# Band scores of a local-attention block: from one 128-row matmul per head pair with zero-filled queries to two 64x64 tiles of the TensorE array

## The chip, the core and the metric

The kernel runs on one core of one Trainium2 chip. The metric is device microseconds of one execution; lower is better. The value for the kernel before is the median of three runs. The trace that is read here comes from one further execution of the same program, taken by the hardware profiler.

## What is computed

Three parts follow each other: an attention with a downsampled and a local branch, and two MLPs. In the local branch a query sees only the seven keys around it (three on each side), which is the "band".

```
# attention: B=4, H=8, S=576, D=64, factor=4
q_d, k_d, v_d = means of q, k, v over groups of 4 positions      # 144 positions
out_up    = repeat(softmax(q_d k_d^T / sqrt(D)) v_d, 4)
mask      = |i - j| < 4
out_local = softmax(where(mask, q k^T / sqrt(D), -1e9)) v
x  = out_up + out_local             # as 2304 tokens x 512
h  = relu(x @ w_in);  x = (h*h) @ w_out        # 512 -> 2048 -> 512
h  = x @ w_in2;       out = softplus(h) @ w_out2
```

## The kernel before

The 2304 tokens are worked on in five blocks of 8, 6, 8, 8 and 6 units of 64 queries. A unit of 64 queries is a `local` task in the first two blocks (14 tasks), and half of a `direct` task, which works on VectorE without TensorE scores, in the other three. The downsampled branch is made of `pooled` tasks, one for a batch and a pair of heads. The MLP steps are `hidden` (its matmuls write `ph`) and `outputs` (they write `y`); each weight is split into two fp32r parts by ScalarE and VectorE (`raw`, `f`, `r`, `w`) the first time it comes in. The MLP inputs and hidden values are split likewise (`xh` and `xl`, `gh` and `gl`).

The order of the instructions of each engine is fixed when the program is built. Each task is a generator that asks for an engine and names an estimated duration, and `Order.run` always takes the piece that could start first. The scores of a `local` task are entered with 0.86 us of TensorE. DMAs on the SP queue are entered in the planner's estimate of when they land (`order.landed`), which also moves what is planned behind them. SP's DMAs use eight semaphores in turn, and each of them waits until the DMA that used its semaphore before it (eight places back) has landed.

A `local` task for 64 queries and 4 pairs of heads goes: scores `lsc` (TensorE), scaling and mask into `ls` (VectorE), row maximum `ln` (VectorE), exponentials `le` with row sums (ScalarE), sum and reciprocal, scaling, transposes `lpp` (TensorE), their copy `lpt`, product with the values `lav` (TensorE), addition of the upsampled branch `lt` (VectorE), and the split into `xh` and `xl`.

For the scores the two heads of a pair lie on partitions 0 to 63 and 64 to 127. So that one matmul with 128 rows yields both heads, the query tile is block-diagonal: head 0 has its 64 queries in columns 0 to 63 and zeros below, head 1 its queries in columns 64 to 127 and zeros above. The zeros are written once by GpSimd. Queries of one task and one pair (index `w`, eight of them in a tile that serves two tasks) are not adjacent: the tile is stored as query by `w`, so that the stationary operand `q[:, :, w]` steps by eight elements. The moving operand is the 70 keys of the unit, read as 96 columns (`KWP`), of which the last 26 are not used. One fp32 matmul is recorded as two passes, each a weight load and a matmul, so that a task's four matmuls are eight rows of each kind.

The names `first` and `w_first` in rows are the same key and query tiles where they lie in borrowed buffers during the start.

Of the kernel before, what the change touches and what calls it, by code (L numbers as in the profile page):

```python
# [9 lines left out]
F32 = mybir.dt.float32  # L10
# [7 lines left out]
B, H, S, D = 4, 8, 576, 64  # L18
NP = H // 2
# [5 lines left out]
QB = 64  # L25
NBLK = S // QB
NG = B * NBLK
KW = QB + 2 * (FCT - 1)
KWP = 96
KH = SP // 2  # L30
NF = DFF // 128
NEG = -1.0e9
# [22 lines left out]
for run in RUNS:  # L55
    b = run[1] + run[0] * NB
# [24 lines left out]
BUFS = dict(q=2, v=3, s=3, e=4, t=5, vd=2, pt=2, n=6, do=5)  # L81
# [36 lines left out]
class Event:  # L118
    at = None
# [129 lines left out]
def fused_kernel(ctx: ExitStack, tc: tile.TileContext, lq, lk, lv, dqk, dv, cdmask, pqk, pv, wts, cmask, cdiag, cident, out):  # L249
    nc = tc.nc  # L250
    act, dve, pe, sp = nc.scalar, nc.vector, nc.tensor, nc.sync
# [34 lines left out]
    r_up = ring(att, "up", [128, NP, SP], 2)  # L286
    banded = lstack.enter_context(tc.tile_pool(name="banded", bufs=1))
    r_v = ring(banded, "v", [KH, 1024], BUFS["v"])
    qs = [banded.tile([128, 2, 2 * NP * QB], F32, name=f"q{k}", tag=f"q{k}") for k in range(BUFS["q"])]
    ks = [banded.tile([128, 2 * NP * KW + KWP - KW], F32, name=f"k{k}", tag=f"k{k}") for k in range(BUFS["q"])]  # L290
    r_q = Ring(lambda name: qs[len(r_q.taken) % BUFS["q"]], BUFS["q"])
    r_k = Ring(lambda name: ks[len(r_k.taken) % BUFS["q"]], BUFS["q"])
    r_t = ring(banded, "t", [128, NP * QB], BUFS["t"])
    r_h = ring(psum, "h", [128, 512], 2)
    r_y = [ring(psum, f"y{m}", [128, 512], 1) for m in range(4)]
# [2 lines left out]
    order = Order()  # L298
# [130 lines left out]
    for g, (i, j) in enumerate(g_block):  # L429
        p0, p1 = LOCAL[i]  # L430
# [15 lines left out]
    lent, first_bufs = {}, {}  # L446

    def lend():

        for p in range(LENT):  # L450
            k = SLOTS1 - 1 - p
            lent[k] = Host()
            both = wpool.tile([128, 2048], F32, name=f"w_first{k}", tag=f"w{k}")
            x, y = both[:, :1024], both[:, 1024:]
            if p < NP:
                q = x.rearrange("p (a x) -> p a x", a=2)
                nc.gpsimd.memset(q, 0.0)
                first_bufs["q", p] = Guest(q, lent[k])
                first_bufs["v", p] = Guest(y[:KH], lent[k])
            else:  # L460
                first_bufs["pv", 0] = Guest(x[:KH], lent[k])
        for p, r in enumerate((r_xh[1], r_xl[1])):
            b = r.take("first")
            host = Host(b)
            x = b.tile.bitcast(F32).rearrange("p h n -> p (h n)")
            first_bufs["in", 2 + p] = Guest(x[:, :2 * S], host)
            k = x[:, 2 * S:2 * S + 2 * NP * KW + KWP - KW]
            nc.gpsimd.memset(k[:, 2 * NP * KW:], 0.0)
            first_bufs["k", p] = Guest(k, host)

    def take_for(r, kind, at):
        return first_bufs.get((kind, at)) or r.take(kind)
# [22 lines left out]
    def load_tasks():  # L495
        todo = [(mask, cmask)]
        for x, y in ((diag, cdiag), (ident, cident)):
            t = yield "sp", 0.06
            sp.dma_start(out=x, in_=y)
            order.landed(t, 65536)  # L500
        for (kind, at, hp, i, _), ev in zip(tasks, arrived, strict=True):
            if kind == "d":
                continue
            if kind == "l":
                if at % 2 == 0:
                    two = at // 2
                    t = yield "sp", 0.06, *room(r_q, "q", two), *room(r_k, "k", two), *room(r_v, "v", two)
                    bq, bk, bv = (take_for(r, x, two) for r, x in ((r_q, "q"), (r_k, "k"), (r_v, "v")))
                    for x in (bq, bk, bv):
                        x.left = 2  # L510
                    for hh in range(2):
                        p0 = 64 * hh
                        sp.dma_start(out=bq.tile[p0:p0 + 64, hh, :], in_=lq[at // 2, p0:p0 + 64])
                        order.landed(t, 128 << 10)
                        t = yield "sp", 0.06
                    sp.dma_start(out=bk.tile[:, :2 * NP * KW], in_=lk[at // 2])
                    there = order.landed(t, 256 * NP * KW * 4)
                    t = yield "sp", 0.06
                    sp.dma_start(out=bv.tile[:KW], in_=lv[at // 2])
                    vthere = order.landed(t, KW * 4096)  # L520
                ev.buf = bq, bk, bv, at % 2
                ev.at = there
                ev.v.at = vthere
            else:
                two = at * NP + hp
                t = yield "sp", 0.06, *room(r_in, "in", two)
                ev.buf = take_for(r_in, "in", two)
                sp.dma_start(out=ev.buf.tile, in_=pqk[at * NP + hp])
                ev.at = order.landed(t, 128 * 4 * 2 * S)
                late = i in DIRECT  # L530
                t = yield "sp", 0.06, *room(r_in if late else r_v, "pv", two)
                ev.v.buf = take_for(r_in if late else r_v, "pv", two)
                ev.v.tile = ev.v.buf.tile[:KH, :1024]
                sp.dma_start(out=ev.v.tile, in_=pv[at * NP + hp])
                ev.v.at = order.landed(t, KH * 4096)
                if todo:
                    t = yield "sp", 0.06
                    sp.dma_start(out=mask, in_=cmask)
                    order.landed(t, 128 * 12 * KW)
                    todo = []  # L540
# [110 lines left out]
    def local(g, banks, ev, pace):  # L651

        b, blk = divmod(g, NBLK)
        i, j = g_block[g]
        t = yield "pe", 0.86, ev, pace, banks, r_s, r_e, r_n, r_t
        sc, s, e, n, o = bank(banks, "lsc"), r_s.take("ls"), r_e.take("le"), r_n.take("ln"), r_t.take("lt")
        bq, bk, bv, at = ev.buf
        q = bq.tile.rearrange("p a (q w) -> p (a q) w", w=2 * NP)
        sc4 = sc.tile[:, :NP * KWP].rearrange("p (h k) -> p h k", h=NP)
        for h in range(NP):  # L660
            w = at * NP + h
            pe.matmul(sc4[:, h, :], q[:, :, w], bk.tile[:, w * KW:w * KW + KWP],  # L662
                      start=True, stop=True)
        used_once(t, bq, bk)
        t = yield "dve", t_dve(280)
        var = 0 if blk == 0 else 2 if blk == NBLK - 1 else 1
        s3 = s.tile[:, :NP * KW].rearrange("p (h k) -> p h k", h=NP)
        dve.scalar_tensor_tensor(
            out=s3, in0=sc4[:, :, :KW], scalar=1.0 / D ** 0.5,
            in1=mask[:, var, :].unsqueeze(1).to_broadcast([128, NP, KW]), op0=ALU.mult, op1=ALU.add)  # L670
        sc.free = t
        t = yield "dve", t_dve(280)
# [315 lines left out]

    with tc.manual_schedule():
        lend()  # L990
        for x in qs + ks:
            nc.gpsimd.memset(x, 0.0)
        act.preload_act_table_set("natural_log_exp_and_others")
        order.spawn(load_tasks(), -100)
        order.spawn(load_weights(), 0, 8.0)
# [21 lines left out]
def _layout(q, k, v, moe_w_in, moe_w_out, moe2_w_in, moe2_w_out):  # L1017
# [9 lines left out]
    kp[..., halo:halo + S] = kt  # L1027
    vs = np.zeros((B, S + 2 * halo, NP, 128), f4)
    vs[:, halo:halo + S] = np.asarray(v, f4).reshape(B, NP, 2, S, D).transpose(0, 3, 1, 2, 4).reshape(B, S, NP, 128)
    lq = np.zeros((NG // 2, 128, QB, 2, NP), f4)  # L1030
    lk = np.zeros((NG // 2, 128, 2, NP, KW), f4)
    lv = np.zeros((NG // 2, KW, 2, NP * 128), f4)
    for b in range(B):
        for i in range(NBLK):
            g = b * NBLK + i
            at = g // 2, slice(None), g % 2
            lq[g // 2, :, :, g % 2] = qt[b, :, :, i * QB:(i + 1) * QB].transpose(1, 2, 0)
            lk[at] = kp[b, :, :, i * QB:i * QB + KW].transpose(1, 0, 2)
            lv[at] = vs[b, i * QB:i * QB + KW].reshape(KW, NP * 128)
    pqk = np.concatenate([qt.reshape(B * NP, 128, S), kt.reshape(B * NP, 128, S)], axis=2)  # L1040
# [55 lines left out]
```

## Time and profile before

| | |
|---|---|
| median of 3 runs | 935.39 us (934.44 to 937.53) |
| the profiled execution | 939.24 us, of which the span from the first to the last instruction is 937.5 us and 1.74 us lie around it |
| busy in the span | PE 911.1 us, weight loads 786.4, DVE 641.8, ACT 508.9, POOL 76.9 |
| HBM traffic | 179.49 MB moved, mean 191 GB/s |
| `lsc` in the chain that ended last | 2% of the span |

PE is TensorE's matmuls, PEld its weight loads, DVE is VectorE, ACT ScalarE, POOL GpSimd, SP the queue that issues most DMAs. A busy time counts an instruction from start to end, and matmuls overlap in the pipeline, so the pace of PE is read from one start to the next. In rows of a timeline the first number is the start and the second the stretch until the last of the merged instructions ended; the bracket gives the idle time ahead and what ended it.

### The profile page before, as it was taken

The numbers are of one execution on the slowest core, as the hardware profiler recorded it, in microseconds if no ns is written. First come the engines' busy times: TensorE is split into PE (matmuls) and PEld (weight loads), VectorE is DVE, ScalarE is ACT, GpSimd is POOL, SyncE is SP. The second block draws the span as 40 slices with busy tenths as digits, with TensorE's granted clock in tenths as the row PEclk, the third lists the DMA queues.
The fourth block names the chain that finished last, engine by engine and source line by source line (L and its number), as shares of the span: only waits on it lengthen the run. The fifth ranks groups of instructions, "written<-read, shape, count | busy, mean of one in ns | idle before, by whom it ended". The sixth has DMA issues, their size and how long they took to land.

```text
span 937.5 us, 12449 instructions
## 1 busy us (share of the span) xinstructions
PE 911.1 (97%) x4416; PEld 786.4 (84%) x4416; DVE 641.8 (68%) x1105; ACT 508.9 (54%) x1141; POOL 76.9 (8%) x146
## 2 busy tenths in 40 slices
PE   4899999999999999999999999999999999999998
PEld 3777888999888877898888888888999888988886
DVE  3768889889999989998797998997211225223222
ACT  3657677667687877654444544443333325444443
POOL 2000000000000000021111112110220011010000
PEclk9969999999999999999999999999999999999999
DMA  8826977986685667378776587661772154123101
GB/s 210 235 75 209 285 258 233 326 278 232 213 306 195 225 239 263 139 259 289 252 257 203 164 275 260 218 212 51 248 248 89 45 165 150 46 90 128 41 0 46
DMA packets 50202, 179.49 MB, mean 191 GB/s; under 512 B 5874, under 2 KB 6258, under 8 KB 50140
## 3 DMA queue, kind: packets, MB, share of 16 engines
q1 hardware_dynamic: 31132, 109.48, 34.8%
q0 software_dynamic: 19008, 69.21, 22.8%
q8 instruction: 35, 0.57, 0.2%
q14 instruction: 27, 0.22, 0.1%
HBM read 140.40 MB, written 38.27 MB: 191 GB/s over the span
## 4 chain that ended last, share of the span: by engine, by line
PE 82%; DVE 9%; DMA 5%; ACT 2%; issue 1%; POOL 0%; SPq 0%; ACTq 0%; POOLq 0%; DVEq 0%
PE ph L870 37%; PE y L924 36%; DMA raw<-wts 3%; DMA first<-lk 3%; PE lsc L662 2%; PE pqk L566 2%; PE ppo L631 1%; PE lav L699 1%; DVE vd L626 1%; DVE f L378 1%; PE psc L589 1%; DVE f L382 1%; DVE gl L319 1%; DVE w L319 1%; PE lpp L691 1%
## 5 line engine op out<-in xcount | busy, mean ns | idle before, releaser
L870 PE MATMUL ph<-xh,w 128*128 128x512 f32 (+2 forms) x1304 | 398.4, 368 | 1.2 <-DVE g L893 1.2
L870 PEld LDWEIGHTS ph<-xh,w 128*128 128x128 f32 x1304 | 242.0, 189 | 33.1 <-DVE g L893 2.3
L870 PE MATMUL ph<-xl,w 128*128 128x512 f32 (+2 forms) x652 | 238.3, 365 | 0.2 <-DVE xl L319 0.2
L924 PE MATMUL y<-gh,w 128*128 128x512 f32 (+2 forms) x656 | 200.2, 367 | 0.0
L924 PE MATMUL y<-w,gh 128*128 128x512 f32 x576 | 179.6, 393 | 0.0
L319 DVE TENSOR_TENSOR gl<-g,gh 128x512 fp32r<-128x512 f32 (+2 forms) x163 | 102.0, 626 | 89.4 <-ACT gh L304 88.4
L870 PEld LDWEIGHTS ph<-xl,w 128*128 128x128 f32 x652 | 123.1, 189 | 15.9 <-DVE xl L319 0.4
L413 POOL DMA_DIRECT2D w<-wdram x132 | 70.1, 534 | 793.9 <-ACT g L887 387.6
L924 PEld LDWEIGHTS y<-gh,w 128*128 128x128 f32 x656 | 121.1, 188 | 14.4 <-issue 0.3
L924 PEld LDWEIGHTS y<-w,gh 128*128 128x128 f32 x576 | 106.7, 188 | 20.6
L924 PE MATMUL y<-gl,w 128*128 128x512 f32 (+2 forms) x328 | 119.1, 363 | 0.0
L924 PE MATMUL y<-w,gl 128*128 128x512 f32 x288 | 112.9, 392 | 0.2 <-DVE gl L319 0.2
L893 DVE SCALAR_TENSOR_TENSOR g<-ph,g 128x512 f32<-128x512 f32 (+2 forms) x81 | 50.8, 628 | 90.4 <-ACT g L891 90.3
L304 ACT ACTIVATE gh<-g 128x512 fp32r<-128x512 f32 (+2 forms) x125 | 71.6, 572 | 70.9 <-PE y L924 51.9
L887 ACT ACTIVATE g<-ph 128x512 f32<-128x512 f32 (+2 forms) x81 | 44.5, 549 | 116.7 <-PE ph L870 107.8
L882 ACT ACTIVATE g<-ph 128x512 f32<-128x512 f32 (+2 forms) x82 | 44.5, 543 | 113.3 <-PE ph L870 92.9
L924 PEld LDWEIGHTS y<-gl,w 128*128 128x128 f32 x328 | 61.7, 188 | 7.1 <-issue 0.3
L924 PEld LDWEIGHTS y<-w,gl 128*128 128x128 f32 x288 | 54.0, 188 | 12.5 <-DVE gl L319 1.0
L369 ACT ACTIVATE f<-raw 128x512 f32<-128x512 f32 x64 | 42.5, 666 | 19.9 <-DMA raw<-wts 11.3
L306 DVE CAST gh<-g 128x512 fp32r<-128x512 f32 (+2 forms) x38 | 15.6, 411 | 49.5 <-PE y L924 43.5
L762 DVE TENSOR_TENSOR prod<-dqk 128x896 f32<-128x896 f32 x44 | 47.7, 1085 | 1.3 <-DMA dqk<-dqk 1.0
L885 ACT ACTIVATE g<-g 128x512 f32<-128x512 f32 (+2 forms) x82 | 47.4, 578 | 1.9
(103 smaller groups left out, 1035.0 us busy)
## 6 DMA issues: line engine op xcount, KB each, us to landing
w<-wdram POOLq DMA_DIRECT2D x132, 512.0 KB, 4.2
raw<-wts SPq DMA_DIRECT2D x64, 512.0 KB, 5.3
wdram<-w SPq DMA_DIRECT2D x64, 512.0 KB, 5.7
dqk<-dqk SPq DMA_DIRECT2D x11, 896.0 KB, 8.2
in<-pqk SPq DMA_DIRECT2D x14, 576.0 KB, 4.8
dv<-dv SPq DMA_DIRECT2D x11, 640.0 KB, 3.9
out<-o SPq DMA_DIRECT2D x18, 256.0 KB, 2.5
pv<-pv SPq DMA_DIRECT2D x15, 288.0 KB
```

What stands on the lines that cost most here:

```text
L304: act.activation(out=out, in_=in_, func=AF.Copy, scale=scale)
L319: dve.tensor_tensor(out=out, in0=whole, in1=high.bitcast(F32), op=ALU.subtract)
L369: act.activation(out=f.tile, in_=high.bitcast(F32), func=AF.Abs, scale=REBIAS)
L413: nc.gpsimd.dma_start(out=weights[slot][:, half], in_=wdram[c, half])
L566: pe.matmul(src, ident, x4[:, :, :, k], start=(k == 0), stop=(k == FCT - 1))
L762: dve.tensor_tensor(out=p4, in0=k4[:, :, tok:tok + TAPS, :], in1=q4[:, tok].unsqueeze(2).to_broadcast([128, 2, TAPS, D]), op=ALU.mult)
L870: pe.matmul(ph.tile[:, :n], w, y, start=(k == 0), stop=(k == len(prs) - 1))
L882: act.activation(out=o, in_=h, func=AF.Relu)
L885: act.activation(out=o, in_=o, func=AF.Square)
L887: act.activation(out=o, in_=h, func=AF.Abs)
L893: dve.scalar_tensor_tensor(out=o, in0=h, scalar=0.0, in1=o, op0=ALU.max, op1=ALU.add)
L924: pe.matmul(o, wt, y, start=(begin and k == 0), stop=(end and k == 2))
```

## The change: two 64x64 tiles, contiguous queries, 70 keys

The zeros, the padding of the keys and the GpSimd memsets are dropped. Each head's scores become a matmul of its own: 64 stationary rows (the head's dimensions) by 64 query columns, over 70 moving key columns. Head 0 uses partitions 0 to 63 for its operands and its output, head 1 partitions 64 to 127, so that the two are different 64x64 tiles of the array; both write the same PSUM bank. The 64 queries of a set now lie side by side. The queries of two tasks come in one DMA of 128 partitions in place of two of 64. What VectorE reads of the scores is as many elements as before.

```diff
-    qs = [banded.tile([128, 2, 2 * NP * QB], F32, name=f"q{k}", tag=f"q{k}") for k in range(BUFS["q"])]
-    ks = [banded.tile([128, 2 * NP * KW + KWP - KW], F32, name=f"k{k}", tag=f"k{k}") for k in range(BUFS["q"])]
+    r_q = ring(banded, "q", [128, 2 * NP * QB], BUFS["q"])
+    r_k = ring(banded, "k", [128, 2 * NP * KW], BUFS["q"])
...
-                    for hh in range(2):
-                        p0 = 64 * hh
-                        sp.dma_start(out=bq.tile[p0:p0 + 64, hh, :], in_=lq[at // 2, p0:p0 + 64])
-                        order.landed(t, 128 << 10)
-                        t = yield "sp", 0.06
-                    sp.dma_start(out=bk.tile[:, :2 * NP * KW], in_=lk[at // 2])
+                    sp.dma_start(out=bq.tile, in_=lq[at // 2])
+                    order.landed(t, 256 << 10)
+                    t = yield "sp", 0.06
+                    sp.dma_start(out=bk.tile, in_=lk[at // 2])
...
-        q = bq.tile.rearrange("p a (q w) -> p (a q) w", w=2 * NP)
-        sc4 = sc.tile[:, :NP * KWP].rearrange("p (h k) -> p h k", h=NP)
+        q = bq.tile.rearrange("p (w q) -> p w q", q=QB)
+        sc4 = sc.tile[:, :NP * KW].rearrange("p (h k) -> p h k", h=NP)
         for h in range(NP):
             w = at * NP + h
-            pe.matmul(sc4[:, h, :], q[:, :, w], bk.tile[:, w * KW:w * KW + KWP],
-                      start=True, stop=True)
+            for p in (slice(0, 64), slice(64, 128)):
+                pe.matmul(sc4[p, h], q[p, w], bk.tile[p, w * KW:w * KW + KW], start=True, stop=True)
...
-            out=s3, in0=sc4[:, :, :KW], scalar=1.0 / D ** 0.5,
+            out=s3, in0=sc4, scalar=1.0 / D ** 0.5,
...
-        for x in qs + ks:
-            nc.gpsimd.memset(x, 0.0)
```

On TensorE the order of all instructions stays as it was, and only the scores take another form. Before, the last three `local` tasks of the first block stand ahead of the first MLP step like this:

```order
L699 MATMUL lav<-lpt,w_first_92 128x128 x4
L662 MATMUL lsc<-k_81,w_first_92 128x96 x4
L662 MATMUL lsc<-k_82,w_first_94 128x96 x8
L870 MATMUL ph<-xh,w_83 128x256
L870 MATMUL ph<-xl,w_83 128x256
```

With the change the same place reads:

```order
L690 MATMUL lav<-lpt,w_first_86 128x128 x4
L654 MATMUL lsc<-k,w_first_86 64x70 x8
L654 MATMUL lsc<-k,w_first_87 64x70 x16
L861 MATMUL ph<-xh,w_79 128x256
L861 MATMUL ph<-xl,w_79 128x256
```

Each of the three tasks has eight matmuls of half the rows and columns in place of four, at the same place between `lav` and `ph`.

On the SP queue the loads of the first pair of tasks stand behind those of the first pooled tasks. Before:

```order
L534 DMA pv<-pv 72x1024
L513 DMA w_first_88<-lq 64x512 x2
L516 DMA first<-lk 128x560
L519 DMA w_first_88<-lv 70x1024
L528 DMA first<-pqk 128x1152
```

With the change:

```order
L525 DMA pv<-pv 72x1024
L504 DMA w_first_84<-lq 128x512
L507 DMA first<-lk 128x560
L510 DMA w_first_84<-lv 70x1024
L519 DMA first<-pqk 128x1152
```

One DMA fewer stands ahead of the keys, with as many bytes, and what follows moves up one place in the turn of the eight semaphores.

VectorE's list is the same for its first 196 rows. Then, at the last tasks of the second block, some fifty rows come in another order, since the planner's times of the loads moved. Before:

```order
L710 TENSOR_TENSOR lt<-lav,up 64x256 x2
L319 TENSOR_TENSOR w_1298<-f,w_1298 128x512
L306 CAST gh<-g 128x512
L319 TENSOR_TENSOR xl<-lt,xh 128x4x64
L319 TENSOR_TENSOR gl<-g,gh 128x512
L668 SCALAR_TENSOR_TENSOR ls<-lsc,mask 128x280
```

With the change:

```order
L701 TENSOR_TENSOR lt<-lav,up 64x256
L303 CAST w_1335<-f 128x512
L701 TENSOR_TENSOR lt<-lav,up 64x256
L659 SCALAR_TENSOR_TENSOR ls<-lsc,mask 128x280
L303 CAST xh<-lt 128x4x64
```

The mask of the next scores now stands ahead of the split of the task before. Over the whole program VectorE has two `xh` casts and one `lpt` copy more, and two `gh` casts and one `part` copy less; ScalarE the reverse. Behind this place the lists agree again.

## Rows read from the trace of the kernel before

**Rows 1.** The page: busy time of the engines and their shares of the span.

```profile
PE 911.1 (97%) x4416; PEld 786.4 (84%) x4416; DVE 641.8 (68%) x1105; ACT 508.9 (54%) x1141; POOL 76.9 (8%) x146
```

**Rows 2.** Windows: stretch: its length, each engine's busy us (instructions), PEclk, DMA share, GB/s.

```profile
60.00:142.00 82.00, 81.61 (x422) 66.73 (x422) 67.24 (x158) 58.45 (x196) 0.00 (x0) 0.97 0.71 226
142.00:232.00 90.00, 89.83 (x501) 85.71 (x500) 81.03 (x154) 62.17 (x125) 0.00 (x0) 1.00 0.78 268
232.00:358.40 126.40, 123.06 (x581) 102.52 (x579) 119.91 (x208) 96.86 (x211) 0.00 (x0) 1.00 0.69 243
358.40:937.50 579.10, 574.79 (x2736) 494.36 (x2736) 338.46 (x509) 259.47 (x495) 70.11 (x132) 1.00 0.49 163
```

**Rows 3.** The chain in order of time around 350 us: start, us, what.

```profile
349.54 5.79 DMA raw<-wts
...
357.67 0.70 DVE g L893
...
358.42 3.06 PE ph L870 x12
```

**Rows 4.** The view of line 662 (the scores): who waited for it, us, times.

```profile
  DVE ls L668: 6.0, 7
```

**Rows 5.** Weight loads by form: rows*columns, operand, count, busy us, mean ns.

```profile
L662 PEld LDWEIGHTS lsc<-k,q 128*128 128x128 f32 x48 | 11.8, 332 | 0.1
...
L691 PEld LDWEIGHTS lpp<-ident,le 128*70 128x70 f32 x56 | 7.3, 134 | 1.7 <-issue 1.0
L699 PEld LDWEIGHTS lav<-lpt,v 70*128 70x128 f32 x48 | 6.2, 191 | 0.4
```

**Rows 6.** Timeline of PE between 100 and 119 us.

```profile
100.78 0.90 PE L589 MATMUL psc<-qkd,qd 128*96 128x144 f32 x6
101.52 2.07 PE L662 MATMUL lsc<-k,q 128*128 128x96 f32 x8
103.37 0.47 PE L870 MATMUL ph<-xh,w 128*128 128x512 f32 x1
...
115.16 0.41 PE L617 MATMUL ppp<-ident,pe 96*72 96x96 f32 x3
115.41 1.08 PE L699 MATMUL lav<-lpt,v 70*128 70x128 f32 x8
116.33 2.04 PE L662 MATMUL lsc<-k,q 128*128 128x96 f32 x8
118.15 0.48 PE L924 MATMUL y<-gh,w 128*128 128x512 f32 x1
```

**Rows 7.** Timeline of PE between 35 and 62 us.

```profile
35.38 1.65 PE L589 MATMUL psc<-qkd,qd 128*96 128x144 f32 x6
36.83 0.69 PE L617 MATMUL ppp<-ident,pe 96*72 96x96 f32 x3
...
52.25 3.79 PE L699 MATMUL lav<-lpt,w_first 70*128 70x128 f32 x16
55.83 5.86 PE L662 MATMUL lsc<-k,w_first 128*128 128x96 f32 x24
61.40 0.56 PE L870 MATMUL ph<-xh,w 128*128 128x256 f32 x1
```

**Rows 8.** Timeline of all engines in the start.

```profile
28.92 2.19 PE L662 MATMUL lsc<-first,w_first 128*128 128x96 f32 x8 [1.92 <-DMA first<-lk]
...
43.00 0.45 DVE L668 SCALAR_TENSOR_TENSOR ls<-lsc,mask 128x280 f32<-128x280 f32 x1 [1.32 <-PE lsc L662]
...
46.40 1.91 DVE L626 TENSOR_REDUCE vd<-pv 72x256 f32<-72x1024 f32 x1
...
48.45 2.26 PE L631 MATMUL ppo<-ppt,vd 72*128 72x288 f32 x4 [1.96 <-DVE ln L682]
```

**Rows 9.** Two windows of the start, columns as in rows 2.

```profile
3.00:28.00 25.00, 13.10 (x50) 10.95 (x50) 12.90 (x23) 9.91 (x40) 4.29 (x8) 1.00 0.94 226
...
57.00:60.00 3.00, 3.00 (x14) 3.00 (x14) 2.25 (x7) 1.34 (x5) 0.00 (x0) 0.50 0.00 0
```

More of the change, by code (lines that the diff above doesn't have):

```diff
@@ L28 @@
 KW = QB + 2 * (FCT - 1)
-KWP = 96
 KH = SP // 2
@@ L288, in fused_kernel @@
     r_v = ring(banded, "v", [KH, 1024], BUFS["v"])
-    qs = [banded.tile([128, 2, 2 * NP * QB], F32, name=f"q{k}", tag=f"q{k}") for k in range(BUFS["q"])]
-    ks = [banded.tile([128, 2 * NP * KW + KWP - KW], F32, name=f"k{k}", tag=f"k{k}") for k in range(BUFS["q"])]
-    r_q = Ring(lambda name: qs[len(r_q.taken) % BUFS["q"]], BUFS["q"])
-    r_k = Ring(lambda name: ks[len(r_k.taken) % BUFS["q"]], BUFS["q"])
+    r_q = ring(banded, "q", [128, 2 * NP * QB], BUFS["q"])
+    r_k = ring(banded, "k", [128, 2 * NP * KW], BUFS["q"])
     r_t = ring(banded, "t", [128, NP * QB], BUFS["t"])
@@ L455, in lend @@
             if p < NP:
-                q = x.rearrange("p (a x) -> p a x", a=2)
-                nc.gpsimd.memset(q, 0.0)
-                first_bufs["q", p] = Guest(q, lent[k])
+                first_bufs["q", p] = Guest(x[:, :2 * NP * QB], lent[k])
                 first_bufs["v", p] = Guest(y[:KH], lent[k])
@@ L466, in lend @@
             first_bufs["in", 2 + p] = Guest(x[:, :2 * S], host)
-            k = x[:, 2 * S:2 * S + 2 * NP * KW + KWP - KW]
-            nc.gpsimd.memset(k[:, 2 * NP * KW:], 0.0)
-            first_bufs["k", p] = Guest(k, host)
+            first_bufs["k", p] = Guest(x[:, 2 * S:2 * S + 2 * NP * KW], host)
     def take_for(r, kind, at):
@@ L1029, in _layout @@
     vs[:, halo:halo + S] = np.asarray(v, f4).reshape(B, NP, 2, S, D).transpose(0, 3, 1, 2, 4).reshape(B, S, NP, 128)
-    lq = np.zeros((NG // 2, 128, QB, 2, NP), f4)
+    lq = np.zeros((NG // 2, 128, 2, NP, QB), f4)
     lk = np.zeros((NG // 2, 128, 2, NP, KW), f4)
@@ L1036, in _layout @@
             at = g // 2, slice(None), g % 2
-            lq[g // 2, :, :, g % 2] = qt[b, :, :, i * QB:(i + 1) * QB].transpose(1, 2, 0)
+            lq[at] = qt[b, :, :, i * QB:(i + 1) * QB].transpose(1, 0, 2)
             lk[at] = kp[b, :, :, i * QB:i * QB + KW].transpose(1, 0, 2)
```

## The prediction, as it was made before the run

> **What bounds the kernel now.** I read the page first: PE is busy for 911.1 of 937.5 us, the next engine, DVE, for 641.8 [rows 1]. That says TensorE, but the share is an average, so I cut the span into four stretches [rows 2]. From 358 us on PE is busy for 574.8 of 579.1 us and DVE for 338.5: there TensorE alone counts, and the change touches nothing in it. From 232 to 358 us DVE is busy for 119.9 of 126.4 us, so that only 6.5 us of it are idle, and the chain of waits up to 358.42 runs over loads of weights and VectorE (`raw`, then `g`, then `ph`) [rows 3]. Ahead of that, from 60 to 232 us, PE is packed (171.4 of 172 us) and DVE idles for 14.8 and 9.0 us. All 14 tasks that the change touches lie before 142 us, eight of them before 61 us. So a gain is made where PE is packed, has to pass a stretch in which VectorE is the bound, and is then kept to the end.
>
> **What the scores cost.** A task's scores are eight passes. From their start to the start of what follows is 1.85 us at 101.52 and 1.82 us at 116.33, 0.23 us a pass [rows 6]. Three tasks at 55.83 take 5.57 us for 24 passes, again 0.23 [rows 7], although the granted clock is 0.50 there [rows 9], the level of 1.2 GHz. Other matmuls follow the clock: `psc` with 144 columns takes 0.242 us a pass at 35.38 [rows 7] and 0.123 at 100.78 [rows 6], `lav` 0.224 and 0.115. So it is not the array that sets the 0.23 us. The weight loads tell what does: those of `lsc`, whose 128 columns step by eight elements, take 332 ns, those of `lav`, 128 columns side by side, 191 [rows 5]. I read it that the stepped read of the queries is the bound. The `psc` rows at 35.38 also show the lower level of the clock, as slow as at 57, though the column of the windows [rows 9] reads 1.00 in the start; I trust the durations.
>
> **What they will cost.** The stepped read goes, and each task has 16 passes of 64 weight columns and 70 moving columns. By `psc`, 0.123 us for 144 columns, a pass streams 60 ns at 2.4 GHz and 118 ns at 1.2 GHz. A load of 64 side by side fits under it: `lav` holds a load of 128 in its 0.115 us. The trace has no tiled matmul, so the price has two ends. If the two heads of a pair run at once, 8 x 60 ns = 0.48 us a task; if one after the other, 16 x 60 = 0.96; if every pass costs as much as the shortest in the trace, `ppp` with 0.25 us for three, 16 x 83 ns = 1.33. I take the middle of the first two, 0.72, since the passes of one head stand one behind the other and can only overlap where the heads change. To this comes the change of the array's form, twice a task. When `y` starts at 118.15, 0.22 us of the scores (2.04 less 1.82) are still in flight [rows 6]; if they have to end first, on both sides, that is 0.44 us; nothing at the least, and I take 0.3. A rule for it is in the Trainium skill, TensorEngine Tiling (Array Packing), Tiling Modes: changing the tiling mode, not just the tile, drains the array. By that rule the full 0.44 us would count, and the sum below would be 0.8 us smaller for the six later tasks. No run here shows it so far.
>
> **Six tasks from 100 to 142 us**, at the full clock: 1.84 - 1.02 = 0.82 us each, 4.9 us in all. Bounds: 1.84 - 0.48 = 1.36 each, 8.2 us; 1.84 - 1.77 = 0.07 each, 0.4 us.
>
> **The start.** Four terms, in order.
> - The keys: at 28.92 PE waits 1.92 us for `lk` [rows 8]. One DMA fewer stands ahead of it, and it is let in one place earlier, but the bytes are the same and the DMA engines are 0.94 busy from 3 to 28 us [rows 9]. Between 0 and 1.92; I take 0.4, near the lower end.
> - Its scores, at the low clock: 8 x 118 ns = 0.94 us or 16 x 118 = 1.89, in the middle 1.42, with the change of form 1.72, against 1.86. Gain 0.15 (between -0.5 and 0.9).
> - At 43.00 DVE waits 1.32 us for the scores; what is late behind it is `vd` at 46.40, and PE waits for VectorE 1.96 us at 48.45 [rows 8]. Two tasks at the full clock stand ahead, which give 1.64, so all of the 1.32 is won (at least 0.14).
> - The three tasks at 55.83, at the low clock, with one change of form: 24 x 118 ns = 2.83 us or 48 x 118 = 5.66, in the middle 4.25, with 0.3 it is 4.55, against 5.57. Gain 1.0 (between -0.5 and 2.7).
>
> The start gives 2.9 us (between -0.9 and 6.8). What is late there next is VectorE, at 48.45.
>
> **Edits at nothing.** The memsets: GpSimd is off the chain, and the first `lq` is held by the order of SP's queue as much as by them; if they hold it, that is inside the 1.92 us above. The mask step on VectorE reads as many elements. The rows that change engine (two casts each way, one copy each way) are even, and their cover is DVE's idle time from 142 to 232 us; without it a copy of 512 columns more ahead of 358 us costs about 0.6 us.
>
> **What arrives.** PE has 2.9 + 4.9 = 7.8 us at 142 (between -0.5 and 15.0). To keep it up to 358 us VectorE must be earlier as well. It waits for the scores seven times, 6.0 us in all [rows 4], and that goes first; its idle time of 23.8 us from 60 to 232 can give more, but part of that waits for loads. I take 80%, 6.2 us, which is close to those 6.0. The sum against the profiled execution is 939.24 - 6.2 = 933.0 us; the median of the runs lies 3.85 us below the profiled one, so 935.39 - 6.2 = 929.2 us.
>
> **Rivals.**
> - *One after the other.* If two tiles can't work at once, a task takes 0.96 + 0.3 us: 0.58 each, 3.5 us for the six; the start gives the 0.4 and the 1.16 of the waits and loses 0.7 at the low clock (2.19 against 1.86, and 5.96 against 5.57). Of 4.4 us 80% is 3.5: 931.9. For it speaks that both heads write the same bank; against it that they write other partitions of it. The Trainium skill has such a rule, TensorEngine Tiling (Array Packing), Restrictions and Gotchas: different row tiles can't use the same PSUM bank at the same time. The two heads here are different row tiles, so by that rule this rival holds; against it, the Trainium skill, TensorE: Matmul & The Clock Gate, Part 3 (Packing small matmuls), lets tiles of different rows run together. No row decides it.
> - *Given back.* VectorE has 6.5 us of idle time from 232 to 358 us [rows 2] and does not get earlier than now, because loads of weights set its pace (5.79 us of one are in the chain at 349.54 [rows 3]). Then PE waits longer ahead of 358.42 and at most 2 us are left: 933.4 to 935.4. Against it: what VectorE loses waiting for the scores is idle time before 142 us.
> - *Slower: loads not hidden.* If the load of a tile's next pass can't start until its own matmul has ended, a pass costs a load and a matmul in a row: 134 ns, as `lpp` with 70 columns [rows 5], and about 0.25 us (`ppp`, 0.41 less two passes of 83 ns [rows 6]), 0.38 us. With the heads overlapping, 8 x 0.38 = 3.1 us a task, 1.2 more than now; over 14 tasks 17 us: 952. It decides from 0.23 us for a pair of passes on. Against it: in the whole trace loads are hidden, 786.4 us of them under 911.1 us of matmuls [rows 1].
> - *More than I take.* Both heads at once all through and no drain: 8.2 + 6.8 = 15.0 us, of which 80%: 923.4.
>
> **How the numbers follow.** Chances: my forecast 0.50, with its own range from 926 to 932; one after the other 0.20; given back 0.15; slower 0.07; more than I take 0.08. The measurement tells about 0.3% from no change, 2.8 us, so faster ends at 932.6. Faster: 0.48 of the forecast, 0.15 of the second, the 0.08, 0.71. Slower: 0.07 and 0.03 from the third case, where the new order on VectorE costs as well, 0.10. Same: 0.19. The range of 8 in 10 runs from 924.5 to 935.4: it leaves out the loads that are not hidden and the top of the gains.
>
> **What would show it.** The 14 `lsc` groups: about 1.0 us from their start to the next start at full clock; 0.48 means that heads run at once, 0.96 that they don't, and over 1.84 the slower rival. The wait of `ls` for `lsc`, now 6.0 us, should nearly go. The first `ph` should start at about 58.5 us in place of 61.40, and the `ph` that ends the VectorE stretch at 352 in place of 358.42. If the first is early and the second is not, the gain was given back. I am wrong if the clock stays at 0.50 longer, because PE idles longer ahead of 48 us: each us of `lav` at the low level costs half a us.

## The result and the profile after

The changed kernel takes 926.16 us (median of 4 runs, 922.56 to 927.25), against 934.91 us (934.17 to 937.53) for the kernel before, measured beside it: ratio 0.9895, interval 0.9872 to 0.9917 (the two medians alone give 0.9906). Forecast were 929.2 us, 924.5 to 935.4. The profiled execution takes 927.25 us, its span is 925.5.

The page, and windows that answer to [rows 1] and [rows 2]; the cut at 345.90 is the `ph` that stood at 358.42 before, while the cut at 142 is the same time and not the same work:

```profile
PE 896.2 (97%) x4528; PEld 767.0 (83%) x4528; DVE 641.4 (69%) x1105; ACT 508.4 (55%) x1141; POOL 70.0 (8%) x136
```

```profile
60.00:142.00 82.00, 79.89 (x507) 62.63 (x507) 74.13 (x170) 62.61 (x195) 0.00 (x0) 1.00 0.78 255
142.00:220.00 78.00, 76.92 (x428) 74.51 (x427) 68.85 (x128) 53.05 (x103) 0.00 (x0) 1.00 0.79 271
220.00:345.90 125.90, 123.45 (x585) 103.31 (x583) 120.77 (x208) 97.90 (x213) 0.00 (x0) 1.00 0.70 245
345.90:925.50 579.60, 574.73 (x2736) 494.30 (x2736) 338.39 (x509) 259.35 (x495) 69.85 (x132) 1.00 0.49 163
```

The last stretch is 579.6 us long against 579.1, with the same work. All of the gain lies ahead of 345.90. There TensorE is no longer packed: from 60 to 142 us it idles for 2.1 us (0.4 in [rows 2]), and VectorE is busy for 74.1 of 82 us where it was for 67.2. The chain around 346 us (start, us, what) has the same links as [rows 3], 12.5 us earlier:

```profile
336.65 6.17 DMA raw<-wts
...
345.15 0.70 DVE g L884
...
345.90 3.04 PE ph L861 x12
```

TensorE's timeline from 119 to 126 us shows two groups of scores, one task and two tasks together:

```profile
119.71 0.71 PE L654 MATMUL lsc<-k,q 64*64 64x70 f32 x16
120.35 0.50 PE L915 MATMUL y<-gh,w 128*128 128x512 f32 x1
...
122.77 0.39 PE L915 MATMUL y<-gl,w 128*128 128x512 f32 x1
122.99 0.39 PE L915 MATMUL y<-gh,w 128*128 128x512 f32 x1
123.31 1.20 PE L654 MATMUL lsc<-k,q 64*64 64x70 f32 x32
124.44 0.50 PE L915 MATMUL y<-gh,w 128*128 128x512 f32 x1
```

From start to next start a task takes 0.64 us (1.82 to 1.85 in [rows 6]) and two take 1.13. The second task adds 0.49 us, 31 ns a pass; what is left of the first, 0.15 us, is all that the change of form behind a group and the filling of the pipeline cost. The change ahead of a group lies before its first start: the `y` at 122.99 takes 0.32 us to the start of the scores, the one at 122.77 only 0.22 to its successor, so that some 0.1 us comes on top. The same timeline in the start, with the bracket for the idle time ahead:

```profile
24.93 0.71 PE L654 MATMUL lsc<-first,w_first 64*64 64x70 f32 x16 [0.51 <-DMA first<-lk]
...
42.58 2.26 PE L622 MATMUL ppo<-ppt,vd 72*128 72x288 f32 x4 [0.64 <-DVE ln L673]
...
46.38 3.79 PE L690 MATMUL lav<-lpt,w_first 70*128 70x128 f32 x16
50.09 3.07 PE L654 MATMUL lsc<-k,w_first 64*64 64x70 f32 x48
53.09 0.58 PE L861 MATMUL ph<-xh,w 128*128 128x256 f32 x1
```

The third task's scores start 3.99 us earlier than in [rows 8], the block of three 5.74 earlier and takes 3.00 us in place of 5.57 [rows 7], and the first `ph` comes 8.31 us earlier. No row of VectorE waiting for `lsc` is left (7 waits, 6.0 us, in [rows 4]): the view of line 654 lists only one later weight load.

```profile
who waited for it (us, times):
  PEld ppo L622: 0.5, 1
```

So the gain of the profiled execution builds up in three steps: 8.3 us at the first `ph`, 11.7 us at the first `ph` of 384 columns (156.48 before, 144.78 now, where the second block's MLP begins), 12.0 us at the end. The two medians differ by 8.75 us; the profiled execution of before was 4.33 us above the 934.91 and that of after 1.1 above its median, which makes the other 3.

### The profile page after: what moved, and what is told of

Its sections match the earlier page's. It is cut to its first block, busy times and chain, and to the rows that moved or that the text cites. A ratio compares the mean times of both kernels' runs of the same rounds, so it can differ in the third digit from the quotient of the medians.

```text
span 925.5 us, 12634 instructions
## 1 busy us (share of the span) xinstructions
PE 896.2 (97%) x4528; PEld 767.0 (83%) x4528; DVE 641.4 (69%) x1105; ACT 508.4 (55%) x1141; POOL 70.0 (8%) x136
## 4 chain that ended last, share of the span: by engine, by line
PE 70%; DVE 15%; DMA 8%; ACT 4%; issue 2%; SPq 0%; ACTq 0%; DVEq 0%
PE ph L861 33%; PE y L915 32%; DMA raw<-wts 5%; PE pqk L557 2%; DVE f L375 2%; DVE vd L617 2%; DVE gl L316 1%; DVE w L316 1%; DMA w_first<-lv 1%; DVE f L379 1%; DMA first<-lk 1%; DVE f L372 1%; DVE prod L789 1%; ACT f L366 1%; PE ppo L622 1%
## 5 line engine op out<-in xcount | busy, mean ns | idle before, releaser
L876 ACT ACTIVATE g<-g 128x512 f32<-128x512 f32 (+2 forms) x82 | 47.4, 578 | 1.9
L880 ACT ACTIVATE g<-g 128x512 f32<-128x512 f32 (+2 forms) x81 | 47.2, 583 | 2.1
```

The costliest lines, as they stand in the source:

```text
L876: act.activation(out=o, in_=o, func=AF.Square)
L880: act.activation(out=o, in_=o, func=AF.Exp, scale=-1.0)
```

## The experiments

Theory A: the one load for the queries and the shorter scores make the whole gain. Rivals: the dropped memsets, the new order on VectorE and ScalarE, and the clock of the start. Of the scores it was open whether the step, the tiles or the alternating heads made them short.

All profiled executions in one table (third = start of the third task's scores; first `ph`; `ph` of 384 columns; span; in us of the profiled execution. Median, number of runs and ratio to the kernel before measured beside it):

| kernel | third | first `ph` | 384 `ph` | span | median (runs) | ratio, interval |
|---|---|---|---|---|---|---|
| before | 28.92 | 61.40 | 156.48 | 937.5 | 934.41 to 934.91 in four series | |
| changed | 24.93 | 53.09 | 144.78 | 925.5 | 926.16 (4) | 0.9895, 0.9872 to 0.9917 |
| two_loads | 27.05 | 55.73 | 146.71 | 925.5 | 927.08 (4) | 0.9915, 0.9896 to 0.9934 |
| memsets | 23.64 | 51.34 | 141.78 | 920.9 | 923.20 (4) | 0.9880, 0.9861 to 0.9899 |
| thrice_early | 23.22 | 54.75 | 146.38 | 925.7 | 927.64 (9) | 0.9931, 0.9911 to 0.9951 |
| thrice_late | 24.83 | 52.15 | 145.70 | 925.2 | 927.01 (4) | 0.9917, 0.9892 to 0.9941 |
| all_back | 25.88 | 56.58 | 151.28 | 930.2 | 934.00 (12) | 0.9990, 0.9975 to 1.0005 |
| old_plan | 23.29 | 51.32 | 141.92 | 921.1 | 924.01 (6) | 0.9889, 0.9863 to 0.9914 |
| new_plan | 27.10 | 58.30 | 156.59 | 936.9 | 936.00 (12) | 1.0014, 1.0000 to 1.0027 |
| one_matmul | 24.33 | 51.37 | 142.11 | 924.6 | 930.19 (10) | 0.9961, 0.9932 to 0.9990 |
| stepped | 23.78 | 49.80 | 140.53 | 919.5 | 926.76 (6) | 0.9909, 0.9877 to 0.9940 |
| heads_apart | 23.16 | 51.63 | 142.41 | 922.4 | 926.58 (6) | 0.9915, 0.9885 to 0.9944 |
| twice_early | 24.15 | 49.48 | 140.72 | 920.6 | 923.37 (4) | 0.9889, 0.9866 to 0.9913 |
| fillers | 24.57 | 53.16 | 149.50 | 928.2 | 929.06 (6) | 0.9936, 0.9913 to 0.9960 |

All kernels but the first are the changed one with an edit, except new_plan. The kernels near the changed one scatter by some 4 us at the first `ph`, and by more in their times, so small differences in one column say little; where an edit costs is read inside its own trace. A profiled execution is one of the runs and need not lie at their median: that of stepped took 921.29 us, the lowest of six.

**The loads** (two_loads):

```diff
-                    sp.dma_start(out=bq.tile, in_=lq[at // 2])
+                    for p in (slice(0, 64), slice(64, 128)):
+                        sp.dma_start(out=bq.tile[p], in_=lq[at // 2, p])
```

> The changed kernel with the queries of two tasks loaded by two DMAs of 64 partitions again, at the same place of SP's list; nothing else differs. Theory A (the loads: one DMA fewer per pair of tasks brings the keys earlier, and that is about half of the 8.3 us that the first MLP step gained): the third group of scores starts at 27 to 29 us in place of 24.93, the first ph at 56 to 57 in place of 53.09, the time is 3 to 4 us longer, about 930. Rival B (the loads land as before, the start was gained by the shorter scores and the missing memsets): all three stay within 1 us of the changed kernel, 926.

SP's timeline around the second pair of tasks, in the changed kernel:

```profile
12.19 0.33 SPq L504 DMA_DIRECT2D w_first<-lq  x1
13.05 0.33 SPq L507 DMA_DIRECT2D first<-lk  x1
```

and in two_loads:

```profile
12.46 1.41 SPq L505 DMA_DIRECT2D w_first<-lq  x2
14.26 0.34 SPq L508 DMA_DIRECT2D first<-lk  x1
```

and in the kernel before, the keys:

```profile
15.33 0.35 SPq L516 DMA_DIRECT2D first<-lk  x1
```

The queries go in at nearly the same time (12.19 and 12.46), but the keys behind them 0.86 us later in the one and 1.80 in the other. The third task's scores need these keys, and start 2.1 us later than in the changed kernel; the last wait in front of them is named as the keys in the changed kernel, in two_loads the trace names none. Over the whole table the third group stands between 23.2 and 24.9 us in the ten kernels with one load and between 25.9 and 28.9 in the four with two: means 24.0 and 27.2, a difference of 3.2 us. In two_loads the first `ph` is 2.6 us later, a little less than expected. In the time of the kernel alone this can't be told from the scatter: 927.08 us, not the 930 expected.

**The memsets** (memsets), GpSimd writing zeros to the query buffers of the start before the loads:

```diff
+                nc.gpsimd.memset(x, 0.0)
```

> The changed kernel with GpSimd's four memsets of the borrowed query tiles put back ahead of their loads (3.6 us of GpSimd); the tiles are overwritten by the loads, so the values are as before. If the memsets held the loads back (rival C), the first load of keys is issued about 0.8 us later, the third group of scores 1 to 4 us later than 24.93, and the time is 1 to 4 us longer. If they were only beside the path (theory A), less than 0.5 us changes anywhere.

Nothing in the start is later than in the changed kernel, and the ratio is no higher. The first `ph` is 1.8 us earlier, which is more than the 0.5 expected but within the scatter. The memsets cost nothing that can be seen.

**The length of the scores, early and late** (thrice_early, thrice_late): the scores are issued three times with the same values, in the eight tasks of the first block (`i == 0`) or the six of the second (`i == 1`).

```diff
-        for h in range(NP):
...
+        for _ in range(3 if i == 0 else 1):
+            for h in range(NP):
...
```

> The changed kernel with each score matmul of the eight tasks of the start issued three times (1.6 us a task at the full clock, against 1.84 before; 9 us for the block of three if the clock is at its lower level). Theory L (the length of the scores carries the start): the first ph starts at 57 us or later, the time is 4 us or more longer than the changed kernel's. Rival W (what counts is that TensorE stays at the higher clock, which more matmuls bring about, as when each was issued twice): the granted clock is 1.00 from 35 to 60 us, the ph starts at 50 to 53, and the time is not longer than 926.

> The changed kernel with each score matmul of the six tasks of the second block issued three times (same values), which brings a task's scores from 0.64 us back to about 1.6, 5.8 us more of TensorE in all; the eight tasks of the start are left alone. Theory A (VectorE sets the pace from about 90 us on, and of the 7.2 us that six tasks gained only 2.9 arrived): the ph of 384 columns that starts at 145.85 comes 1 to 3 us later, the time is 1 to 3 us longer. Rival D (TensorE sets the pace up to there): 5 to 6 us later, 932.

In thrice_early the block of three takes 5.54 us (49.21 to 54.75), as long as before, and from the third group to the first `ph` it is 31.5 us: 32.5 before, 28.2 in the changed kernel. So the shorter scores, not the loads, give most of the 4.3 us behind the third group; 2.5 of the 3.4 us that thrice_early takes back lie in the block itself. Neither expectation came true: the first `ph` is earlier than 57 and later than 53, and the time is 1.5 us longer, not 4.

The path from the third group to the `ppo` (a product of the downsampled branch) ahead of the block is another matter: 19.53 us before (28.92 to 48.45), 17.65 in the changed kernel (24.93 to 42.58), but 18.48 in thrice_early and 17.35 in all_back below, which have the long scores. What also differs on this path is the clock, as `lav` shows in the kernel before and in the changed one:

```profile
33.68 1.92 PE L699 MATMUL lav<-lpt,w_first 70*128 70x128 f32 x8
```

```profile
27.01 1.13 PE L690 MATMUL lav<-lpt,w_first 70*128 70x128 f32 x8
```

The 1.92 us are the lower level, the 1.13 the upper one, and all_back has 1.13 as well. The durations of the kernel before stay at the lower level until about 37 us (the column of the windows reads 1.00 there; the durations are trusted here, as in the prediction). How much of the 1.88 us on this path is the price of a pass and how much the clock, no run separates.

Late the added passes hardly arrive. The stretch from the first `ph` to the `ph` of 384 columns, as a window of the changed kernel, of thrice_late and of the kernel before:

```profile
53.09:144.78 91.69, 89.13 (x542) 68.64 (x541) 81.25 (x191) 67.66 (x221) 0.00 (x0) 0.99 0.73 236
```

```profile
52.15:145.70 93.55, 92.77 (x736) 73.94 (x733) 81.67 (x191) 68.57 (x221) 0.00 (x0) 1.00 0.71 232
```

```profile
61.40:156.48 95.08, 94.69 (x494) 77.48 (x493) 80.91 (x188) 67.71 (x214) 0.00 (x0) 0.98 0.72 228
```

The passes added in thrice_late take 5.9 us (four tasks at 1.62 and a pair at 3.09, for 0.64 and 1.13); they make the stretch only 1.9 us longer, and TensorE's idle time falls from 2.6 to 0.8 us. The largest piece of that idle time in the changed kernel, 1.19 us ahead of the `ph` at 133.33, ends with a weight that ScalarE splits (`w`); the other two have no such wait. Against before, the six tasks save TensorE 6 x 1.20 = 7.2 us, and the stretch is 3.4 shorter; 2.2 of the rest is idle time of TensorE (2.56 against 0.39). VectorE's work is the same 81 us in all three, 89% of the stretch now. Of the last 1.6 us, some 0.1 ahead of each of the five groups is the change of form; the rest is not accounted for.

**All back** (all_back): two loads, the memsets, and the scores three times in all 14 tasks.

```diff
+                nc.gpsimd.memset(x, 0.0)
...
+                    for p in (slice(0, 64), slice(64, 128)):
+                        sp.dma_start(out=bq.tile[p], in_=lq[at // 2, p])
...
+        for _ in range(3):
```

> The changed kernel with the three named causes put back together: the queries come in two loads again, GpSimd writes its zeros again, and the scores of all 14 tasks are issued three times (same values), about 1.6 us a task at the full clock and 3.0 at the low one, near the length they had before. Theory A (loads and length of the scores make the whole gain): the first `ph` starts at 57 to 61 us, the first 128x384 `ph` at 150 to 156, and the median is 931 to 935 us. Rival (something else, such as the new order on VectorE, makes part of it): 929 us or less, with the first `ph` below 56.

TensorE's timeline:

```profile
25.88 1.69 PE L657 MATMUL lsc<-first,w_first 64*64 64x70 f32 x48 [1.76 <-DMA first<-lk]
...
49.72 6.93 PE L657 MATMUL lsc<-k,w_first 64*64 64x70 f32 x144
```

The wait for the keys is back (1.76 us, 1.92 in [rows 8]), and the time with it: 934.00 us, 0.999 of the kernel before. The first `ph` is a little earlier than expected, 56.58. With new_plan and memsets, which rule the order and the memsets out, loads and length of the scores are enough to make the whole gain, to within the interval (0.9975 to 1.0005). How the gain divides among them the times don't tell: alone, two_loads, thrice_early and thrice_late add 0.0020, 0.0036 and 0.0022 to the ratio, each with an interval as wide, and all together, in all_back, 0.0095.

**The order** (old_plan, new_plan): the planner's entries exchanged, the loads themselves left. In old_plan VectorE's and ScalarE's lists are those of before, in new_plan the kernel before has those of the changed one.

```diff
-                    order.landed(t, 256 << 10)
-                    t = yield "sp", 0.06
+                    for _ in range(2):
+                        order.landed(t, 128 << 10)
+                        t = yield "sp", 0.06
```

> The changed kernel with the planner's entries of before for the query loads (two of half the size in place of one), while one load is issued: VectorE's and ScalarE's lists are those of the kernel before. Theory A: the order counts for nothing, the first 128x384 `ph` within 1 us of 144.8 and the median within 1 us of 926.2. Rival (the new order lets VectorE be earlier): that `ph` 1 to 3 us later and the median up to 3 us higher.

> The kernel before, with its own scores, zeros and two query loads, but with the planner's entry of the changed kernel, so that VectorE's and ScalarE's lists are those of the changed kernel. Theory A: 934 to 936 us, the first `ph` at 60 to 61.5 and the group of the third task's scores at 27 to 29 us. Rival (the order makes part of the gain): 931 to 933.

old_plan keeps the gain (0.9889), new_plan wins nothing (1.0014). The `ph` of 384 columns of old_plan is 2.9 us earlier, not within 1 us as expected, but against the rival. The order is no part of the gain. new_plan is also a second profile of the start of before: third group 27.10, first `ph` 58.30 (60 to 61.5 were expected), against 28.92 and 61.40. Some 2 to 3 us of what the two first profiles show in the start are thus scatter, and it is gone by the `ph` of 384 columns (156.59 and 156.48).

**What makes the scores short** (one_matmul, stepped, heads_apart). one_matmul goes back to one matmul of 128 rows with zeros, but contiguous queries and 70 keys; its query loads carry the zeros, twice the bytes.

```diff
-            for p in (slice(0, 64), slice(64, 128)):
-                pe.matmul(sc4[p, h], q[p, w], bk.tile[p, w * KW:w * KW + KW], start=True, stop=True)
+            pe.matmul(sc4[:, h], q[:, w], bk.tile[:, w * KW:w * KW + KW], start=True, stop=True)
```

> The changed kernel without tiles: 128 rows and zero-filled queries again, but side by side, and with the zeros in DRAM, so that one load brings 512 KB of queries in place of 256; 70 keys. Theory S: a pass takes as long as lav's, 0.115 us at the full clock, a task 0.92 to 1.0 us, half of what it took before the change, so that the step and not the tiles is most of the gain in the scores. Rival T: 1.84 stays. The loads of the start are 7% more bytes, so the second keys come 1 to 3 us later than 24.93, and the time is 2 to 4 us longer than the changed kernel's.

stepped has the tiles, with the queries stored as before:

```diff
-        q = bq.tile.rearrange("p (w q) -> p w q", q=QB)
+        q = bq.tile.rearrange("p (q w) -> p w q", q=QB)
```

> The changed kernel with the queries stored interleaved again, so that the 64 stationary columns of each tile step by eight elements; the order of all instructions is the same. Theory S (the stepped read of the queries set the 0.23 us of a pass, about 1.8 ns a column): a load takes 115 ns at either clock, a task 0.92 us if the loads of the two heads run at once and 1.84 if they don't, against 0.64; the time is 1 to 4 us longer than the changed kernel's. Rival T (the form of the matmul set it, 128 rows with half zeros): a task stays at 0.64 us.

heads_apart issues the eight passes of head 0 and then those of head 1:

```diff
-        for h in range(NP):
-            w = at * NP + h
-            for p in (slice(0, 64), slice(64, 128)):
+        for p in (slice(0, 64), slice(64, 128)):
+            for h in range(NP):
+                w = at * NP + h
```

> The changed kernel with a task's four matmuls of head 0 first and the four of head 1 behind them; same matmuls. Theory O (two tiles overlap, but only where the head changes, which now happens once in 16 passes in place of seven times): a task at the full clock takes 16 x 60 = 0.96 us and a little in place of 0.64. Rival P (40 ns is the pace of short passes as such, whatever tile they are in): 0.64 stays. The whole time changes by less than 2 us either way.

TensorE's timelines of the three, in this order, at the full clock (2.4 GHz):

```profile
95.67 1.01 PE L653 MATMUL lsc<-k,q 128*128 128x70 f32 x8
96.48 0.48 PE L860 MATMUL ph<-xh,w 128*128 128x512 f32 x1
```

```profile
102.57 1.18 PE L654 MATMUL lsc<-k,q 64*64 64x70 f32 x16
103.68 0.50 PE L915 MATMUL y<-gh,w 128*128 128x512 f32 x1
```

```profile
104.75 1.00 PE L654 MATMUL lsc<-k,q 64*64 64x70 f32 x16
105.69 0.50 PE L915 MATMUL y<-gh,w 128*128 128x512 f32 x1
```

The weight loads of the changed kernel and of stepped, from the views of their line 654 (duration ns min/median/max):

```profile
L654 PEld LDWEIGHTS lsc<-k,q x96: 129/133/136, 93.1 to 124.2; 64*64 64x64 f32 x96
```

```profile
L654 PEld LDWEIGHTS lsc<-k,q x96: 191/213/215, 88.9 to 121.6; 64*64 64x64 f32 x96
```

Without the step the old form takes 0.81 us in place of 1.84 (0.92 to 1.0 expected). It also reads 70 key columns in place of 96, but 96 columns need 82 ns a pass by `psc`, less than the 101 ns that a pass takes here, so the step is by all likelihood the 1.0 us. With the step the tiles take 1.11 us, 69 ns a pass, and a load of 64 columns 213 ns against 133. So either the contiguous queries or the tiles alone make the scores much shorter, and their gains don't add up: 1.03 us by the first, 0.73 by the second, 1.20 by both. In the time of the kernel stepped can't be told from the changed kernel (926.76 and 926.16 us; 1 to 4 us more were expected).

With the heads apart a task takes 0.94 us, as expected. Single passes show why. Two views of the changed kernel (windows 119.88:119.94 and 119.94:120.00) and two of heads_apart (104.90:104.97 and 104.98:105.04); x is the number of passes that have started:

```profile
119.71 0.40 PE L654 MATMUL lsc<-k,q 64*64 64x70 f32 x6
119.71 0.46 PE L654 MATMUL lsc<-k,q 64*64 64x70 f32 x8
```

```profile
104.75 0.40 PE L654 MATMUL lsc<-k,q 64*64 64x70 f32 x3
104.75 0.46 PE L654 MATMUL lsc<-k,q 64*64 64x70 f32 x4
```

In the time that 70 columns need by the estimate from `psc` (60 ns), two passes start where the heads alternate, and only one where the passes of one head stand alone. That the average of heads_apart, 59 ns, is so near to 60 is partly chance: it holds the 0.15 us of the ends, and the heads overlap in the middle of the group there too. At the lower level of the clock its block of three takes 3.76 us (47.87 to 51.63), 78 ns a pass, where 118 would be needed without any overlap.

one_matmul's median of 930.19 us is above what 0.17 us a task explain, and its runs lie between 924.2 and 935.9 us; its query loads have twice the bytes, but they did not bring the keys later (third group at 24.33, where 1 to 3 us later were expected). What makes its time longer was not separated.

**The clock** (twice_early, fillers): in the start of the changed kernel the granted clock is at the lower level for a while. twice_early issues the scores of the first block twice; fillers does so with its `lpp` and `lav` too.

```diff
+        for _ in range(2 if i == 0 else 1):
```

> The changed kernel with each score matmul of the eight tasks of the start issued twice, which brings the three tasks ahead of the first MLP step from 3.0 to about 6 us (5.57 in the kernel before) and the others from 0.6 to 1.1 (1.84 before); the loads are left as changed. If the shorter scores carry the start (rival B), the first ph starts at 57 to 58 us in place of 53.09 and the time is 4 us longer; if half is the loads (theory A), the ph comes 3 to 4 us later, since the block of three alone gives 3.0, and the second keys still let the third group start at 24.9.

> The changed kernel in which the eight tasks of the first block issue their scores, transposes `lpp` and products `lav` twice with the same values, so that TensorE idles less in the start. Rival W (the clock at its lower level in the start holds the first `ph` back): the granted clock is 1.00 from 35 to 60 us, the first `ph` comes at 50 or earlier, and the median is 924 or less. Theory A (the start is set by loads and VectorE): the first `ph` at 52 to 55 and the median 926 or more.

The window from 36 to 54 us of the changed kernel, of twice_early and of fillers (the last but two is the granted clock):

```profile
36.00:54.00 18.00, 15.79 (x98) 13.18 (x99) 14.35 (x37) 13.13 (x44) 0.00 (x0) 0.54 0.40 124
```

```profile
36.00:54.00 18.00, 14.90 (x164) 11.83 (x165) 17.52 (x47) 14.54 (x57) 0.00 (x0) 1.00 0.38 111
```

```profile
36.00:54.00 18.00, 16.89 (x228) 15.46 (x227) 15.93 (x43) 12.81 (x43) 0.00 (x0) 1.00 0.39 112
```

And the block of three in fillers:

```profile
50.07 3.16 PE L655 MATMUL lsc<-k,w_first 64*64 64x70 f32 x96
53.16 0.39 PE L864 MATMUL ph<-xh,w 128*128 128x256 f32 x1
```

Both hold 2.4 GHz through this window. In twice_early the first `ph` then comes at 49.48, 3.6 us earlier than in the changed kernel, with twice the scores, against both expectations; but stepped, with no pass more, has it at 49.80, and the times of twice_early and of the changed kernel overlap. In fillers it comes at 53.16, and the median is 929.06, so that the rival falls in the form in which it was put. But fillers could not have shown it: its doubled `lpp` and `lav` take at the upper level as long as the single ones at the lower (1.91 and 3.84 us; 1.91 and 3.79 in the changed kernel). What the clock is worth there shows in twice_early, from the last `ppo` to the block of three:

```profile
41.62 1.21 PE L622 MATMUL ppo<-ppt,vd 72*128 72x288 f32 x4 [1.96 <-DVE ln L674]
...
46.39 3.16 PE L655 MATMUL lsc<-k,w_first 64*64 64x70 f32 x96
```

This takes 4.77 us, in stepped, where the upper level returns at 45 us, 5.57, and 7.51 us in the changed kernel (42.58 to 50.09) and in six others that have the same passes at the lower level. So the clock can make up to 2.7 us of the scatter at the first `ph`. In the kernel before the same path takes 7.38 us (48.45 to 55.83), so that this piece of it is no part of the gain between the two first profiles. fillers costs more behind it too: tasks of the first block still have their `lpp` and `lav` after the first `ph`, and doubled they lengthen a packed stretch. As a cause of the whole gain the clock falls: the mean granted clock of the runs is 0.984 to 0.993 in the changed kernel and 0.986 to 0.996 in the kernel before, as far as its runs list it. No version was found that is faster than the changed kernel by more than the scatter.

## Why the prediction was right, and where its steps were not

- **What bounds the kernel.** Right: the gain lies ahead of 346 us, and the last stretch did not move.
- **The stepped read as the bound of the old scores.** Right, shown by one_matmul and stepped.
- **The price of the new scores** was mis-sized: 0.64 us a task at the full clock in place of 1.02. The step that failed is "in the middle of the first two, 0.72", with its reason that heads overlap only where they change. In the order of issue chosen here the two heads run together all through: 31 ns a pass, half of 60, which is the lower end of 0.48 us; heads_apart shows the case in which they do so only in part. Of the 0.3 us for the change of form at most 0.15 lie behind a group and some 0.1 ahead of it, so that term was about right. The Trainium skill, TensorEngine Tiling (Array Packing), Tiling Modes, states that a change of the tiling mode drains the array. The rows bound what that costs here, some 0.25 us for both changes.
- **The start** gave 8.3 us for 2.9. The term that failed most is the keys, 0.4 us for 4.0. Its upper bound of 1.92, the wait in front of the scores, was no bound: the keys entered the queue 2.3 us earlier, and the work ahead of the wait moved as well (TensorE was done with it at 27.00 before and is at 24.42 now). The path from there to the block of three gave 1.75 (1.47 taken), which may be the price of a pass or the clock, and the block 2.57 (1.0 taken) by the price of a pass. Scatter of 2 to 3 us lies in these numbers, as new_plan shows. The sign of being wrong that was named, a longer stay at the low clock, did not show: the granted clock is 0.50 for 17.1 us in both, from 47.8 to 64.8 us before and from 37.6 to 54.7 now.
- **Six later tasks, and what arrives.** Taken were 4.9 us with 80% kept from 142 to the end. TensorE saved 7.2, but only 3.4 arrived at the `ph` of 384 columns; there thrice_late shows the same weak hold, 1.9 for 5.9. From there to the first `dpp` it is 237.6 us before (156.48 to 394.06) and 236.7 now (144.78 to 381.52), and between 234.9 and 238.7 in the edited kernels: all that came in was kept. So the loss was put in the wrong place: it lies ahead of 146 us, where part of what TensorE saved turned into idle time, and not behind it. (`dpp` are transposes of the `direct` tasks.)
- **The edits at nothing** (memsets, order) cost nothing that can be seen, shown by memsets, old_plan and new_plan.
- **The total.** The profiled gain is 12.0 us for 6.2: the start gave 5.4 more, the six tasks 1.5 less, and behind them 1.6 were taken as lost that were not, and 0.3 came in addition. Of the 12.0 some 3 lie in the scatter of the two profiled executions, so that the median came 3.0 us below the forecast and inside the range. That it came so near is partly luck: the terms missed by 5.4, 1.5 and 1.6 us and did not all miss the same way.
- **The rivals.** One after the other fell: heads overlap (31 ns a pass where one alone needs 60) although they write one bank. The rule in the Trainium skill, TensorEngine Tiling (Array Packing), Restrictions and Gotchas, that different row tiles can't use one PSUM bank at the same time does not hold here, where the two heads write different partitions of the bank. Given back fell, since the 11.7 us at the `ph` of 384 columns are still there at 345.90 (12.5). Loads not hidden fell: passes start every 31 ns though a load takes 133, so loads run beside passes and beside each other. More than I take had the price of the scores nearly right (0.48 for 0.64), and its 923.4 us lies 2.8 below the median and inside the runs (922.56 to 927.25).

## What to carry to other kernels

A stationary operand that is read with a step can cost more than the matmul itself, so look first at the weight loads' duration against those of a contiguous operand of the same shape; storing it contiguously alone took a task's scores from 1.84 to 0.81 us. Two edits that each remove the same cost don't add up, so try them one by one. Small matmuls on different rows of the array pay most when they alternate. A wait in front of an instruction doesn't bound what an earlier load can give, and time saved on the busiest engine arrives only as far as what feeds that engine keeps up. Work that is added to hold the clock up must not cost what the clock gives.

## What the runs showed of the hardware that was not expected

- Two 64x64 tiles on the diagonal of the array that write one PSUM bank run together: 31 to 32 ns a pass in blocks (1.13 us for 32 passes less 0.64 for 16; 3.09 us for 96 passes in fillers), 59 ns when the passes of a head follow each other (heads_apart), with a part of them still overlapping.
- A contiguous load of 64 columns took 133 ns at the full clock, with a step of eight elements 213; of 128 columns 192 (one_matmul) and 332 [rows 5]. The stepped loads hardly changed with the clock, the contiguous ones did (median 223 ns over the last four tasks of the first block of the changed kernel, most of it at the lower level).
- The granted clock fell to 0.50 (1.2 GHz) at 37.6 us of the changed kernel; TensorE had been busy for 5.69 us from 28 to 36 us and for 0.16 from 36 to 37.5. In fillers it was busy for 7.91 and 1.50 us there and the clock stayed at 1.00 (2.4 GHz). But in twice_early TensorE was busy for only 4.34 of 7 us from 39 to 46, with the clock at 1.00 there and behind it: its idle time alone does not tell when the level falls.
